# Gates of the last two token chunks by seven half-block products

## The chip, the cores and the metric

The kernel runs on one core of one Trainium2 chip. The metric is device microseconds (us) of one execution, taken as the median over runs; 255.19 us before the change. Engines are named as the profile names them: PE is TensorE (its weight loads have a row of their own, PEld), DVE is VectorE, ACT is ScalarE, POOL is GpSimd, SP is SyncE, which here only issues transfers.

## The reference

Linear attention over 8 batches of 8 heads, 576 positions and 64 features, followed by a gated feed-forward block over all 4608 tokens:

```
def phi(x):
    return np.where(x > 0, x, np.exp(x) - 1.0) + 1.0
kv  = einsum('bhsd,bhse->bhde', phi(k), v)
z   = sum(phi(k), axis=2)
num = einsum('bhsd,bhde->bhse', phi(q), kv)
den = einsum('bhsd,bhd->bhs', phi(q), z)[..., None] + 1e-06
x   = (num / den) as 4608 tokens x 512
a = x @ w1          # 512 -> 1024
b = x @ w2          # 512 -> 1024
h = a * b @ w3      # 1024 -> 1024
out = h @ w_out     # 1024 -> 512
```

Inputs and output are float32; the kernel multiplies in bf16 and accumulates in float32.

## The kernel before

The product w3 @ w_out is formed once on the chip (tile `wf_sb`), so that behind the gates a * b only one matrix is left. The tokens are treated in nine chunks of 512. Chunk c below 8 holds positions 0 to 511 of batch c; chunk 8 holds the remaining 64 positions of all eight batches ("the tails"). For each chunk there are these steps:

- K, `kv_full`: batch b's kv product, accumulated in PSUM and copied to SBUF by ACT or DVE.
- A, `nat`: the numerators and denominators of 128 tokens (j = 0 to 3), or of the 64 tail positions (j = 4): four matmuls of 130 columns into the one PSUM tile `nd`, then on DVE an addition, a reciprocal and a multiplication into `xn` or `xnr`.
- D, `xt_load`: a transposing transfer, issued by SP, that turns `xn` into `xt` (feature rows, token columns), or a pair of batches' `xnr` into a quarter of `xtr`, which chunk 8 reads.
- F, `f_unit`: one of eight column blocks of 128 gates: four matmuls of 512 columns with w1 into `a_ps` (L343), four with w2 into `b_ps`, an ACT copy of `a_ps` (L348) and a DVE multiplication with `b_ps` into `ab` (L349).
- O, `o_unit`: 128 output tokens: eight matmuls of 512 columns (L500) and a copy by ACT, or by DVE where the step has a plus (L502).
- S and H, stores of two output blocks or one; Q, `o_last`: the last block in two halves of 256 columns (L525), each copied and stored on its own.

What follows what is not left to a scheduler. A string, ORDER, lists all steps; the program is recorded in that order, every engine works through its own instructions in it, and the waits between engines follow from the data and from the reuse of buffers. A plus behind a step moves its copy or its operation to another engine. Transfers are queued on SP and POOL in the same order.

PSUM has eight banks here: four of tag "mm" (the F steps, Q), one each of tags "o" and "u" (the O steps take turns), and two for the tile that `nat` and `kv_full` share. SBUF tiles of tag "ld" (13 buffers of 4 KB per partition) take the loads of k, q and v; behind batch 7's conversion nothing loads into them any more.

The kernel before already has functions for gates by seven products (`ws_make`, `xs_make`, `g_product`, `g_unit`, `g_mul`; steps e, d, G and m), but its ORDER does not use them.

Of the kernel before, what the change touches and what calls it, by code (L numbers as in the profile page):

```python
# [8 lines left out]
F32 = mybir.dt.float32  # L9
BF16 = mybir.dt.bfloat16  # L10
AF = mybir.ActivationFunctionType
ALU = mybir.AluOpType

P = 128
NCH = 512
HN = 256
NQ = 4
# [3 lines left out]
def kernel(  # L21
# [11 lines left out]
    nc = tc.nc  # L33
# [15 lines left out]
    ld = ctx.enter_context(tc.tile_pool(name="ld", bufs=13))  # L49
# [4 lines left out]
    lr = ctx.enter_context(tc.tile_pool(name="lr", bufs=4))  # L54
    xt_p = ctx.enter_context(tc.tile_pool(name="xt", bufs=3))
    ab_p = ctx.enter_context(tc.tile_pool(name="ab", bufs=2))
    ws_p = ctx.enter_context(tc.tile_pool(name="ws", bufs=1))
    sm = ctx.enter_context(tc.tile_pool(name="sm", bufs=3))
    mm_ps = ctx.enter_context(tc.tile_pool(name="mm_ps", bufs=4, space=bass.MemoryType.PSUM))
    o_ps_p = ctx.enter_context(tc.tile_pool(name="o_ps", bufs=1, space=bass.MemoryType.PSUM))  # L60
# [250 lines left out]
    def xt_of(c):  # L311
        if c == B:
            return xtr
        if c not in xts:
            xts[c] = xt_p.tile([P, NJ, KC, P], BF16, tag="xt", name="xt")
        return xts[c]
# [40 lines left out]


    wss, xss, cs_ = [[None] * 4, [None] * 4], {}, {}

    def ws_make(w, i, alt):
        t, s = (w1_sb, w2_sb)[w], wss[w]
        s[i] = ws_p.tile([P, 2, NQ * P], BF16, tag=f"w{w}{i}", name=f"ws{w}{i}")

        def blk(r, h):
            return t[:, 2 * h:2 * h + 2, r * NCH:r * NCH + NQ * P]
        a, b, op = ((lambda: blk(1, 0), lambda: blk(1, 1), ALU.add),
                    (lambda: s[0], lambda: blk(0, 0), ALU.subtract),
                    (lambda: blk(0, 0), lambda: blk(1, 0), ALU.subtract),
                    (lambda: blk(0, 1), lambda: s[1], ALU.subtract))[i]  # L370
        (nc.gpsimd if alt else nc.vector).tensor_tensor(out=s[i], in0=a(), in1=b(), op=op)

    def xs_make(c, i, alt):
        if c not in xss:
            xss[c] = xt_p.tile([P, 4, 2, 2, P], BF16, tag="xs", name="xs", bufs=1)
        x, s = xt_of(c), xss[c]

        def blk(h, r):
            return x[:, 2 * r:2 * r + 2, 2 * h:2 * h + 2]
        a, b = ((lambda: blk(0, 1), lambda: blk(0, 0)), (lambda: blk(1, 1), lambda: s[:, 0]),  # L380
                (lambda: blk(1, 1), lambda: blk(0, 1)), (lambda: blk(1, 0), lambda: s[:, 1]))[i]
        (nc.gpsimd if alt else nc.vector).tensor_tensor(
            out=s[:, i], in0=a(), in1=b(), op=ALU.subtract)

    def g_product(t, c, q, a, m, first):

        for w in range(2):
            for k in range(2):
                if a[0] == 0:
                    l = (w1_sb, w2_sb)[w][:, 2 * a[2] + k, (q + 4 * a[1]) * P:(q + 4 * a[1] + 1) * P]  # L390
                else:
                    l = wss[w][a[1]][:, k, q * P:(q + 1) * P]
                if m[0] == 0:
                    r = xt_of(c)[:, 2 * m[2]:2 * m[2] + 2, 2 * m[1] + k, :]
                else:
                    r = xss[c][:, m[1], :, k, :]
                nc.tensor.matmul(t[:, w], l, r, start=(first and w == 0 and k == 0), stop=(k == 1),
                                 skip_group_check=True)

    def fsm(name):  # L400
        return sm.tile([P, 2, HN], F32, tag="f", name=name, bufs=4)

    def g_unit(c, q, i):
        if c not in abs_:
            abs_[c] = ab_p.tile([P, FC, NCH], BF16, tag="ab", name="ab")
        st = cs_.setdefault((c, q), {})
        a, m, name, first = ((), ((0, 0, 0), (0, 0, 0), "u", True), ((0, 0, 1), (0, 1, 0), "t", True),
                             ((1, 1), (1, 1), "u", False), ((1, 0), (1, 0), "t2", True),
                             ((1, 2), (1, 2), "u", False), ((1, 3), (0, 1, 1), "t2", False),
                             ((0, 1, 1), (1, 3), "u", False))[i]  # L410
        if first:
            pool, tag = (o_ps_p, "ou"[q % 2]) if name == "u" else (mm_ps, "mm")
            st[name] = pool.tile([P, 2, HN], F32, tag=tag, name="g" + name)
        t = st[name]
        g_product(t, c, q, a, m, first)
        if i in (1, 3, 4):
            s = st["s", i] = fsm("gs")
            nc.scalar.copy(out=s, in_=t)
        elif i in (2, 5, 6):
            s = st["c", i] = fsm("gc")  # L420
            nc.vector.tensor_tensor(out=s, in0=st["s", {2: 1, 5: 4, 6: 3}[i]], in1=t, op=ALU.add)
        else:
            s = fsm("ga")
            nc.scalar.copy(out=s[:, 0], in_=t[:, 0])
            nc.vector.tensor_mul(out=abs_[c][:, q + 4, 0:HN], in0=s[:, 0], in1=t[:, 1])

    def g_mul(c, q, i, alt):
        s = cs_[c, q]["c", i]
        f, r = {2: (q, 0), 5: (q + 4, 1), 6: (q, 1)}[i]
        (nc.gpsimd if alt else nc.vector).tensor_mul(  # L430
            out=abs_[c][:, f, r * HN:(r + 1) * HN], in0=s[:, 0], in1=s[:, 1])


    def a_block(c, r, h):
# [124 lines left out]
    x6.0 M7.0 A5.3 D3.1 x7.0 z6.1 F4.0 v6.1+ v6.2 F4.6 A4.4 Z6.0 F4.1 S3.0 F4.4 D5.0 A5.4 y6.0 z6.0  # L559
    F4.3 M7.1 F5.7 x7.2 y7.0 Y7.0 z7.2 L7.1 N7.0 K6+ z7.0 F5.6 F5.0 y7.1 X7.1 X7.0 Z7.0 F5.5 S3.1  # L560
    F5.3 Y7.1 T6.0 R7.1+ Z7.1 A6.3 T7.0 F5.1 O4.2 A6.1 x7.1 O4.1 A6.2 N7.1 z7.1 F5.4 A6.0 F5.2 v7.1
    v7.2+ O4.0 D6.0 D5.1 A6.4 v7.0 O4.3+ S4.1 K7 O5.0 F6.3 S4.0 O5.1 A7.4 F6.5 F6.4 D7.1 F6.1 A7.3
    O5.2 O5.3 A7.1 F6.2 F8.3 A7.0 F8.6 S5.1 F6.6 A7.2 S5.0 F6.0 F6.7 D7.0 O6.3+ O6.2 O6.1 O6.0+ F7.1
    F7.7 F7.2 F8.0 S6.1 F8.7 S6.0 F8.1 F8.5 F7.4 F8.2 F8.4 F7.6 O8.2 F7.5 H8.2 F7.3 F7.0 O8.3 H8.3
    O7.0 O7.1 S7.0 O8.0 O8.1 S8.0 O7.2 H7.2 Q7.3
    """
    GATES = "R6.0<T3.0"
    ctx.enter_context(tc.manual_schedule())
# [8 lines left out]
    def step(s):  # L577
# [5 lines left out]
        if t == "F":  # L583
            f_unit(b, i)
        elif t == "G":
            g_unit(b, i, int(at[1]))
        elif t == "m":
            g_mul(b, i, int(at[1]), alt)
        elif t == "e":
            ws_make(b, i, alt)  # L590
        elif t == "d":
            xs_make(b, i, alt)
        elif t == "O":
            o_unit(b, i, alt)
# [89 lines left out]
```

## Time and profile before

| what | value |
|---|---|
| median of three runs | 255.19 us |
| lowest and highest of them | 254.96 and 255.96 us |
| the profiled execution: time on the device | 254.38 us |
| the profiled execution: span of the profile | 252.6 us |
| transfers in the profiled execution | 49.54 MB, 196 GB/s on average |

The span runs from the first instruction to the end of the last transfer. The 1.8 us between it and the execution's own time lie around the profile. A profile's matmul lasts longer than the distance to the next one, since matmuls are pipelined: what a matmul costs is read from the distance of starts. All rows with a line number (L343) refer to the kernel before.

### The profile page before, as it was taken

To read this page: it belongs to the slowest core of one execution; us is meant where nothing else is said; L and a number is where in the kernel's file an instruction comes from. 1 tells how busy PE (TensorE), PEld (TensorE's weight loads), DVE (VectorE), ACT (ScalarE), POOL (GpSimd) and SP (SyncE) were. 2 spreads that over 40 slices of the span, in tenths; PEclk is the share of its full clock that TensorE was granted. 3 is DMA by queue.
4 is the path that set the end of the run, shared out by engine and by line. 5 is a ranking of instruction groups with operands and counts; after the bars stand their busy time and mean duration, and the time that the engine had idled before them with its cause. 6 is when DMAs were issued, how large, how long until landed. Compare 5 with 4: busy or idle time off the path is not lost.

```text
span 252.6 us, 3848 instructions
## 1 busy us (share of the span) xinstructions
PE 231.3 (92%) x1384; PEld 117.8 (47%) x1400; DVE 156.9 (62%) x350; ACT 116.1 (46%) x179; POOL 48.7 (19%) x82
## 2 busy tenths in 40 slices
PE   0088999999999999998999999999999999999994
PEld 0064564654454544444445445444544444444442
DVE  0548498679998566967886999887235632442300
ACT  2402677357756636719471573645232312323231
POOL 8625469456041050600000000000000000000000
PEclk9999999999999999999999999999999999999999
DMA  6999999999999999999999999656512244000144
GB/s 219 213 229 214 295 272 185 204 255 283 292 232 297 198 273 293 277 274 264 342 303 256 302 219 298 128 98 154 197 23 82 84 84 169 0 0 3 39 149 145
DMA packets 65427, 49.54 MB, mean 196 GB/s; under 512 B 33536, under 2 KB 60416, under 8 KB 65408
## 3 DMA queue, kind: packets, MB, share of 16 engines
q1 hardware_dynamic: 54576, 37.10, 58.6%
q0 software_dynamic: 10688, 12.06, 23.8%
q8 instruction: 11, 0.18, 0.3%
q10 hardware_dynamic: 144, 0.13, 0.1%
q14 instruction: 8, 0.07, 0.1%
HBM read 38.80 MB, written 9.44 MB: 191 GB/s over the span
## 4 chain that ended last, share of the span: by engine, by line
PE 69%; DMA 21%; issue 3%; SPq 2%; DVE 2%; POOL 1%; ACT 1%; ACTq 0%; POOLq 0%
PE a_ps L343 21%; PE b_ps L343 21%; PE o_ps L500 20%; DMA w3b<-in_moe_w_dram 10%; DMA q<-in_q_dram 5%; DMA v<-in_v_dram 3%; PE nd L301 3%; DMA qk32r<-in_k_dram 3%; PE kvp L246 2%; SPq L105 1%; SPq L332 1%; PE o_ps L525 1%; DVE kj L210 1%; PE kvp L250 1%; PE kvp L240 0%
## 5 line engine op out<-in xcount | busy, mean ns | idle before, releaser
L343 PEld LDWEIGHTS <-w_sb 128*128 128x128 bf16 x576 | 55.0, 98 | 63.2 <-issue 1.9
L349 DVE TENSOR_TENSOR ab<-a_sb,b_ps 128x512 bf16<-128x512 f32 x72 | 49.2, 686 | 38.4 <-PE b_ps L343 28.9
L343 PE MATMUL a_ps<-xt,w_sb 128*128 128x512 bf16 x256 | 66.7, 379 | 0.7 <-ACT xt L323 0.5
L343 PE MATMUL b_ps<-xt,w_sb 128*128 128x512 bf16 x256 | 66.7, 379 | 0.2 <-DVE ab L349 0.2
L348 ACT COPY a_sb<-a_ps 128x512 f32<-128x512 f32 x72 | 42.0, 585 | 53.7 <-PE a_ps L343 49.2
L500 PE MATMUL o_ps<-wf_sb,ab 128*128 128x512 bf16 x267 | 62.7, 379 | 0.8 <-issue 0.2
L500 PEld LDWEIGHTS <-ab 128*128 128x128 bf16 x280 | 26.9, 98 | 29.9
L502 ACT COPY o_sb<-o_ps 128x512 f32<-128x512 f32 x29 | 16.8, 586 | 41.8 <-PE o_ps L500 26.4
L307 DVE TENSOR_TENSOR xn<-nd,r 128x512 bf16<-128x512 f32 x32 | 22.1, 691 | 1.1
L180 ACT ACTIVATE e<-k 128x1024 bf16<-128x1024 f32 x16 | 16.6, 1055 | 7.8 <-DMA k<-in_k_dram 7.8
L180 ACT ACTIVATE e<-q 128x1024 bf16<-128x1024 f32 x16 | 16.7, 1055 | 7.4 <-DMA q<-in_q_dram 7.4
L148 PE MATMUL w3p<-ident,w3b 128*128 128x128 bf16 x64 | 5.7, 242 | 13.3 <-DMA w3b<-in_moe_w_dram 13.3
L301 PEld LDWEIGHTS <-qt 128*128 128x128 bf16 (+1 forms) x160 | 11.5, 99 | 11.4 <-issue 2.7
L301 PE MATMUL nd<-kv,qt 128*128 128x130 bf16 (+1 forms) x160 | 15.8, 220 | 0.5 <-ACT kv L255 0.5
L185 DVE TENSOR_SCALAR y<-q 128x1024 bf16<-128x1024 f32 x16 | 11.0, 694 | 8.0 <-DMA q<-in_q_dram 8.0
L155 PE MATMUL wf_ps<-wt_sb,w3t 128*128 128x512 bf16 x61 | 14.8, 379 | 0.7 <-DMA wt_sb<-in_moe_w_out_dram 0.5
L305 DVE TENSOR_SCALAR r<-nd 128x8 f32<-128x8 f32 (+1 forms) x40 | 6.4, 161 | 13.2 <-PE nd L301 12.8
L115 POOL DMA_DIRECT2D qk32r<-in_q_dram x14 | 9.0, 648 | 24.9 <-DMA qt<-qj 11.9
L210 DVE TENSOR_TENSOR qj<-e,y 128x512 bf16<-128x512 bf16 x32 | 12.0, 418 | 0.4 <-ACT e L180 0.3
L185 DVE TENSOR_SCALAR y<-k 128x1024 bf16<-128x1024 f32 x16 | 11.0, 687 | 2.0 <-DMA k<-in_k_dram 1.9
L210 DVE TENSOR_TENSOR kj<-e,y 128x512 bf16<-128x512 bf16 x32 | 11.9, 418 | 0.2
L148 PEld LDWEIGHTS <-w3b 128*128 128x128 bf16 x64 | 4.5, 109 | 14.8 <-DMA w3b<-in_moe_w_dram 14.5
(59 smaller groups left out, 181.7 us busy)
## 6 DMA issues: line engine op xcount, KB each, us to landing
out_dram<-o_sb SPq DMA_DIRECT2D x15, 512.0 KB, 3.7
q<-in_q_dram SPq DMA_DIRECT2D x13, 512.0 KB, 9.2
k<-in_k_dram SPq DMA_DIRECT2D x13, 512.0 KB, 6.4
v<-in_v_dram SPq DMA_DIRECT2D x12, 512.0 KB, 8.9
w3b<-in_moe_w_dram POOLq DMA_DIRECT2D x8, 256.0 KB, 12.2
w_sb<-in_moe_w_dram POOLq DMA_DIRECT2D x8, 256.0 KB, 7.2
q<-in_q_dram POOLq DMA_DIRECT2D x3, 512.0 KB, 11.4
k<-in_k_dram POOLq DMA_DIRECT2D x3, 512.0 KB, 12.4
```

The source lines that it names most:

```text
L148: nc.tensor.transpose(tp[:, kc, :], raw["w3", i // 4][:, i % 4, kc * P:(kc + 1) * P], ident)
L155: nc.tensor.matmul(wfs[i], w3ts[i][:, kc, :], wo_sb[:, kc, :], start=(kc == 0), stop=(kc == FC - 1))
L180: nc.scalar.activation(out=e, in_=x, func=AF.Exp)
L185: (nc.gpsimd if alt else nc.vector).tensor_scalar(out=y, in0=x, scalar1=0.0, scalar2=1.0, op0=ALU.max, op1=ALU.add)
L210: nc.vector.tensor_tensor(out=p[0][:, 2 * g + c].rearrange("p j u d -> p u j d"), in0=e[:, c], in1=y[:, c], op=ALU.min)
L301: nc.tensor.matmul(nd[rows, g, i * 2 * E1:(i + 1) * 2 * E1], w, kvs[b % 2][:, i, g].rearrange("p u e -> p (u e)"), start=True, stop=True)
L307: nc.vector.tensor_tensor(out=dst.rearrange("p (g h) e -> p g h e", g=2), in0=v4[:, :, :, 0:D], in1=r[rows].unsqueeze(3).to_broadcast([n, ...
L343: nc.tensor.matmul(ps, w[:, kc, f * P:(f + 1) * P], xt_of(c)[:, :, kc, :], start=(kc == 0), stop=(kc == KC - 1))
L348: nc.scalar.copy(out=a_sb, in_=a_ps)
L349: nc.vector.tensor_mul(out=abs_[c][:, f, :], in0=a_sb, in1=b_ps)
L500: nc.tensor.matmul(o_ps, ab[:, f, m * P:(m + 1) * P], wf_sb[:, f, :], start=(f == 0), stop=(f == FC - 1))
L502: copy_of(alt)(out=rows_of(c, m // 2)[:, m % 2], in_=o_ps)
```

## The change

The 16 F steps of chunks 7 and 8 are replaced by steps G. With the 1024 gate columns split into two halves of 512, the 512 features into two halves of 256 and the 512 tokens into two halves of 256, a gate matrix is a product of two 2 x 2 block matrices; seven block products with sums of blocks (Strassen, in Winograd's form) give it instead of eight. `g_unit(c, q, i)` does product i (1 to 7) for the column blocks q and q + 4, for w1 and w2 together: 2 x 2 matmuls of 256 columns into one bank. Products 1, 3 and 4 are copied to SBUF by ACT, products 2, 5 and 6 are added on DVE to such a copy, product 7 ends in an ACT copy of the w1 half and a DVE multiplication by the w2 half. `g_mul` (step m) multiplies the two halves of the sums 2, 5 and 6 on DVE. Products 3, 5 and 7 go on accumulating in the bank of product 1, and product 6 in that of product 4.

Steps e form the sums of weight blocks (four each of w1 and w2, 1024 bf16 columns), steps d the sums of xt blocks (four for each of the two chunks, 512 columns); all of them on DVE.

The buffers for these come from the pool of the loads: four tiles for the weight sums, two for the xt sums, and six tiles cut in two for a ring of twelve float32 buffers. Their order of reuse is written out with `ring`.

```
-    ws_p = ctx.enter_context(tc.tile_pool(name="ws", bufs=1))
...
+    spare = {}
+
+    def from_ld(key, shape, dtype):
+        if key not in spare:
+            spare[key] = ld.tile(shape, dtype, tag="ld", name="spare")
+        return spare[key]
...
-        s[i] = ws_p.tile([P, 2, NQ * P], BF16, tag=f"w{w}{i}", name=f"ws{w}{i}")
+        s[i] = from_ld(("w", w, i // 2), [P, 2, 2, NQ * P], BF16)[:, i % 2]
...
-            xss[c] = xt_p.tile([P, 4, 2, 2, P], BF16, tag="xs", name="xs", bufs=1)
+            xss[c] = from_ld(("x", c), [P, 4, 2, 2, P], BF16)
...
+    ring = []
+
     def fsm(name):
-        return sm.tile([P, 2, HN], F32, tag="f", name=name, bufs=4)
+        if not spare.get("ring"):
+            spare["ring"] = True
+            for n in range(6):
+                t = from_ld(("f", n), [P, 2, 2, HN], F32)
+                ring.extend((t[:, 0], t[:, 1]))
+        return ring.pop(0)
...
-            nc.vector.tensor_tensor(out=s, in0=st["s", {2: 1, 5: 4, 6: 3}[i]], in1=t, op=ALU.add)
+            o = st["s", {2: 1, 5: 4, 6: 3}[i]]
+            nc.vector.tensor_tensor(out=s, in0=o, in1=t, op=ALU.add)
+            ring.append(o)
```

A buffer also goes back to the ring behind product 7's multiplication and behind each step m. The order of the steps, from the store S4.1 on; before:

```
S4.1 K7 O5.0 F6.3 S4.0 O5.1 A7.4 F6.5 F6.4 D7.1 F6.1 A7.3
O5.2 O5.3 A7.1 F6.2 F8.3 A7.0 F8.6 S5.1 F6.6 A7.2 S5.0 F6.0 F6.7 D7.0 O6.3+ O6.2 O6.1 O6.0+ F7.1
F7.7 F7.2 F8.0 S6.1 F8.7 S6.0 F8.1 F8.5 F7.4 F8.2 F8.4 F7.6 O8.2 F7.5 H8.2 F7.3 F7.0 O8.3 H8.3
O7.0 O7.1 S7.0 O8.0 O8.1 S8.0 O7.2 H7.2 Q7.3
```

and after:

```
S4.1 e0.0 K7 F6.1 e0.2 O5.0 e0.1 e1.2 S4.0 A7.4 D7.1 e1.0
O5.1 F6.0 d8.0 A7.3 e1.1 O5.2 O5.3 d8.1 d8.2 d8.3 A7.2 G8.0.1 e0.3 G8.1.4 G8.1.1 G8.0.2 e1.3
G8.0.4 G8.0.3 G8.1.3 F6.6 G8.0.5 G8.1.5 m8.0.2 m8.1.5 G8.0.6 F6.5 m8.0.6 G8.1.7 G8.0.7 F6.7
m8.0.5 G8.2.1 G8.3.1 G8.1.6 G8.2.4 G8.2.3 A7.1 G8.3.3 G8.3.4 G8.2.5 S5.1 F6.4 A7.0 G8.3.5 G8.2.7
F6.2 m8.1.6 S5.0 D7.0 G8.3.7 F6.3 m8.3.5 G8.3.6 O6.0+ G8.3.2 d7.0 m8.3.6 O6.1+ d7.1 m8.2.5 d7.3
O6.2+ d7.2 O6.3+ G7.0.1 S6.0 G8.2.6 G8.1.2 G7.1.1 m8.2.6 G7.0.4 m8.1.2 G7.0.3 G7.1.2 G7.1.3
G7.1.4 m8.3.2 G7.0.5 G7.1.5 G7.2.4 S6.1 G8.2.2 G7.0.7 G7.1.7 G7.1.6 G7.0.2 m8.2.2 G7.2.1 G7.3.1
m7.1.2 G7.0.6 m7.1.6 G7.2.3 G7.2.2 G7.3.3 G7.2.5 G7.3.4 G7.3.2 G7.3.5 G7.2.7 G7.3.6 G7.2.6
G7.3.7 m7.0.2 O8.0+ m7.3.2 m7.2.2 O8.1 O8.2 S8.0 O8.3+ m7.0.5 m7.1.5 H8.2 m7.0.6 m7.2.6 m7.3.5
m7.2.5 H8.3 m7.3.6 O7.0 O7.1+ O7.2+ S7.0 H7.2 Q7.3
```

The instructions of every engine ahead of this point are the same in both programs.

More of the change, by code (lines that the diff above doesn't have):

```diff
@@ L425, in g_unit @@
             nc.vector.tensor_mul(out=abs_[c][:, q + 4, 0:HN], in0=s[:, 0], in1=t[:, 1])
+            ring.append(s)
     def g_mul(c, q, i, alt):
@@ L431, in g_mul @@
             out=abs_[c][:, f, r * HN:(r + 1) * HN], in0=s[:, 0], in1=s[:, 1])
+        ring.append(s)
     def a_block(c, r, h):
@@ L561 @@
     F5.3 Y7.1 T6.0 R7.1+ Z7.1 A6.3 T7.0 F5.1 O4.2 A6.1 x7.1 O4.1 A6.2 N7.1 z7.1 F5.4 A6.0 F5.2 v7.1
[L562 to L565, printed above, removed]
+    v7.2+ O4.0 D6.0 D5.1 A6.4 v7.0 O4.3+ S4.1 e0.0 K7 F6.1 e0.2 O5.0 e0.1 e1.2 S4.0 A7.4 D7.1 e1.0
+    O5.1 F6.0 d8.0 A7.3 e1.1 O5.2 O5.3 d8.1 d8.2 d8.3 A7.2 G8.0.1 e0.3 G8.1.4 G8.1.1 G8.0.2 e1.3
[7 more added lines that the diff above has]
+    m7.2.5 H8.3 m7.3.6 O7.0 O7.1+ O7.2+ S7.0 H7.2 Q7.3
     """
```

## The prediction

> **What bounds the kernel now.** I read the page first, then the stretches behind batch 7's kv product, then the chain of waits, then single instructions in order of time.
>
> ```profile
> span 252.6 us, 3848 instructions
> PE 231.3 (92%) x1384; PEld 117.8 (47%) x1400; DVE 156.9 (62%) x350; ACT 116.1 (46%) x179; POOL 48.7 (19%) x82
> ...
> PE   0088999999999999998999999999999999999994
> ...
> DVE  0548498679998566967886999887235632442300
> ...
> PEclk9999999999999999999999999999999999999999
> ```
>
> TensorE (PE) is the full engine from the third slice to the last, and the clock granted is whole all along. VectorE (DVE) falls from 8 and 9 tenths to 2 to 6 tenths from slice 28 (177 us) on. That is where the change begins: the order of steps is the same up to batch 7's kv product (K7), whose last product ends at 178.4 us. Behind that point, in four stretches (columns: bounds, length, then PE, PEld, DVE, ACT, POOL busy us with counts, clock, DMA share, GB/s):
>
> ```profile
> 178.00:189.00 11.00, 10.95 (x60) 5.17 (x59) 3.29 (x7) 3.98 (x8) 0.00 (x0) 1.00 0.30 109
> 189.00:212.00 23.00, 22.89 (x118) 10.95 (x119) 10.17 (x21) 6.16 (x12) 0.00 (x0) 1.00 0.29 92
> 212.00:231.00 19.00, 18.95 (x89) 8.60 (x89) 7.57 (x11) 6.36 (x11) 0.00 (x0) 1.00 0.07 28
> 231.00:249.00 18.00, 17.95 (x91) 8.73 (x90) 2.49 (x4) 5.86 (x10) 0.00 (x0) 1.00 0.34 93
> ```
>
> PE is busy 70.7 of 71 us, while DVE does 23.5 us of work and ACT 22.4. So PE's time in this stretch is the time of the kernel, and a microsecond taken off PE comes off the end, as long as nobody makes it wait. The chain of waits (start, length, what) says the same and prices the products:
>
> ```profile
> 211.00 0.86 PE a_ps L343 x4
> 211.87 0.86 PE b_ps L343 x4
> ...
> 228.27 0.86 PE a_ps L343 x4
> ...
> 247.26 1.76 PE o_ps L525 x16
> ```
>
> From 211.00 to 228.27 us lie 20 groups of four 512-column matmuls back to back: 17.27 / 80 = 0.2159 us each.
>
> **PE's sum.** Removed: sixteen F steps (F7.0 to F7.7, F8.0 to F8.7) of eight 512-column matmuls, 128 x 0.2159 = 27.63 us. Added: for two chunks, four column blocks and seven products, 2 x 2 matmuls of 256 columns, so 224, each with a weight load of its own (224 loads for 128). The 256-column matmul has rows in the last step, Q7.3 (start, length, engine; the length of one is 0.272):
>
> ```profile
> 246.88 1.84 PEld L525 LDWEIGHTS <-ab 128*128 128x128 bf16 x16
> 247.10 1.91 PE L525 MATMUL o_ps<-wf_sb,ab 128*128 128x256 bf16 x16
> ...
> L525 PE MATMUL o_ps<-wf_sb,ab 128*128 128x256 bf16 x16 | 1.9, 272 | 0.0
> L525 PEld LDWEIGHTS <-ab 128*128 128x128 bf16 x16 | 1.6, 98 | 0.4
> ```
>
> Sixteen take 1.91 us, so (1.91 - 0.272) / 15 = 0.1092 us each, with a weight load of 98 ns between each two. 224 x 0.1092 = 24.46. PE's work shrinks by 27.63 - 24.46 = **3.17 us**; by the chain's coarser 1.76 / 16 = 0.110 it would be 2.99.
>
> A load of 98 ns beside a product of 109 leaves little room, so this is the place to ask whether loads are hidden. The rows above say they are; so does a narrower case:
>
> ```profile
> 189.21 0.39 PE L301 MATMUL nd<-kv,qt 128*128 128x130 bf16 x4
> 189.38 3.17 PEld L500 LDWEIGHTS <-ab 128*128 128x128 bf16 x16
> 189.44 3.62 PE L500 MATMUL o_ps<-wf_sb,ab 128*128 128x512 bf16 x15
> ```
>
> Four 130-column products and their four loads pass in 189.44 - 189.21 = 0.23 us, 58 ns a pair. I take loads as free; if they were not, 96 more of them at 98 ns would cost 9.4 us (a rival below). The Trainium skill, page "TensorE: Matmul & The Clock Gate", section "Part 3: Packing small matmuls — row/col tiling", under "The mechanism", says that a weight load overlaps running matmuls only where the two use different row groups; all of these use the full array, so by it every load would stand in series. The two fences disagree with it.
>
> **What the seven products ask of DVE and ACT.** A removed F step has one ACT copy and one DVE product of 128x512, 16 of each. Added per column block: three ACT copies and three DVE adds of 128x512, an ACT copy and a DVE product of 128x256 from PSUM, and three DVE products of 128x256 in SBUF. Their prices:
>
> ```profile
> 166.53 0.69 DVE L307 TENSOR_TENSOR xn<-nd,r 128x512 bf16<-128x512 f32 x1
> 167.14 0.68 DVE L349 TENSOR_TENSOR ab<-a_sb,b_ps 128x512 bf16<-128x512 f32 x1
> ...
> 181.00 0.59 ACT L502 COPY o_sb<-o_ps 128x512 f32<-128x512 f32 x1 [1.63 <-DMA out_dram<-o_sb]
> 181.48 0.59 ACT L348 COPY a_sb<-a_ps 128x512 f32<-128x512 f32 x1
> ...
> 248.23 0.42 DVE L527 COPY o_sb<-o_ps 128x256 f32<-128x256 f32 x1 [10.53 <-DMA out_dram<-o_sb]
> 249.05 0.37 ACT L527 COPY o_sb<-o_ps 128x256 f32<-128x256 f32 x1 [1.12 <-PE o_ps L525]
> ```
>
> A DVE operation of 512 columns lasts 0.69 us, but the next starts after 167.14 - 166.53 = 0.61; ACT's after 0.48. The add has no row (f32 out instead of bf16), nor has the f32 product of two SBUF operands. I price the add like L349: 0.61 in a queue, 0.69 alone. For the 256-column products the nearest row is L527's copy: 0.42 alone, and with the same overlap of 0.08, 0.34 in a queue. The lower end for them is half of that (0.21), the upper end twice (0.85).
>
> Per column block DVE needs 3 x 0.61 + 4 x 0.34 = 3.2 us, and PE 28 x 0.1092 = 3.06. So DVE, idle for two thirds of this stretch before, becomes as costly as PE wherever products follow each other undiluted. ACT needs 3 x 0.48 + 0.29 = 1.7 and has room.
>
> Chunk 8's products are mixed with six F6 steps and two nat steps. From A7.2 to O6.0 the new order has 24 of the 28 products (24 x 4 x 0.1092 = 10.5 us) and 48 + 8 older products (6 x 1.73 + 2 x 0.23 = 10.8), 21.3 us on PE; DVE has 8 adds, 10 small products, 6 L349 and two nat chains of 1.1, with two weight sums: 4.9 + 3.4 + 3.7 + 2.2 + 1.2 = 15.4. It is hidden.
>
> Chunk 7's are not diluted: from G7.0.1 to O8.0 PE has 31 products, 31 x 4 x 0.1092 = 13.54 us, DVE 15 adds, 4 products from PSUM and 7 deferred ones: 15 x 0.61 + 11 x 0.34 = 12.9 us, 95% of PE's. With every operation at its full length it is 15 x 0.69 + 11 x 0.42 = 15.0, and PE would wait 1.4. Each add holds a bank that a later product needs, so at this load some waits come through. Bounds 0 and 1.4; I take 0.3, near the lower end, because the spacing of 0.61 is what back-to-back rows show.
>
> The remaining nine small products of chunk 7 stand on DVE behind O8.0's copy; seven of them behind O8.3's, which waits for PE to finish O8.3. O7.2 reads what they write. From the end of O8.3, DVE needs 0.61 + 7 x 0.34 = 3.0 us and PE gives it O7.0 and O7.1, 2 x 1.73 = 3.45. Cover 0.45; at 0.42 each, 0.1 of a wait; at 0.85 each, 3.1. I take 0.15.
>
> The sums of weights (eight of 1024 columns, bf16) and of xt blocks (eight of 512) go to DVE. For bf16 sums of 512 columns the row is
>
> ```profile
> L210 DVE TENSOR_TENSOR qj<-e,y 128x512 bf16<-128x512 bf16 x32 | 12.0, 418 | 0.4 <-ACT e L180 0.3
> ```
>
> so between 0.42 and 0.84 each for the longer ones, at most 8 x 0.84 + 8 x 0.42 = 10 us in 41 us (178 to 219) where DVE had about 16 us of work before; the six weight sums ahead of chunk 8's first products lie under F6.1, F6.0 and four O5 steps. At nothing, with one exception.
>
> **The step that moves past a queue.** DVE works strictly in order, and d8.0 (first sum of tail blocks) waits there for batch 7's tail transpose, D7.1; behind it stands A7.3's normalisation, and PE's A7.2 waits for that, since nat has one PSUM tile. The rows of before:
>
> ```profile
> 178.40 1.89 PE L500 MATMUL o_ps<-wf_sb,ab 128*128 128x512 bf16 x8
> ...
> 183.68 0.41 PE L301 MATMUL nd<-kv,qt 128*64 128x130 bf16 x4
> ...
> 184.13 0.17 DVE L305 TENSOR_SCALAR r<-nd 64x8 f32<-64x8 f32 x1 [1.31 <-PE nd L301]
> ...
> 184.56 0.69 DVE L307 TENSOR_TENSOR xnr<-nd,r 64x512 bf16<-64x512 f32 x1
> ...
> 185.28 1.19 SPq L332 DMA_TRANSPOSE xtr<-xnr  x1
> ...
> xtr<-xnr SPq DMA_TRANSPOSE x1, 2.4
> ...
> DMA to landing us min/median/max: 2.4/4.4/7.5
> ```
>
> In the new order F6.1 starts at 178.40, A7.4 after two steps of 1.73 at 181.9. DVE is through with F6.1's product at about 180.9 and then has three weight sums, to 182.8; A7.4's chain of 1.15 lets SP issue D7.1 at 184.0, 1.3 us earlier than before. With a landing of 2.4 us d8.0 starts at 186.4 and A7.3's chain ends near 188.0. PE reaches A7.2 after six steps of 1.73 and two of 0.23, at 178.4 + 10.8 = 189.2. So a landing of up to about 3.5 us is covered, and each microsecond beyond it is a microsecond of PE. I take 2.4, the row of this same transfer with the queue quiet around it; S4's two stores stand ahead of D7.1 as before. D7.0, the last xt transpose, is issued some 5 us later than before, behind S5's stores, and still has about 6 us before the first chunk 7 sum is read. Nothing else on SP or POOL moves past a wait that matters.
>
> **Sum.** Against the profiled execution's own time, 254.38 us (its span of 252.6 and 1.8 around it): 254.38 - 3.17 + 0.3 + 0.15 = 251.7. The median of the runs, 255.19, stands 0.8 above that execution, so I forecast **252.5 us**, and 251.7 to 253.9 for this case alone (no wait at all and some noise; up to 1.9 us of waits).
>
> **Rivals.**
> First, VectorE sets the pace of chunk 7's gates. With x more per add the stage costs PE 15x - 0.6 us. For it: 95% load, and add and SBUF product without rows. Against it: L349, with the same operands but the output's type, and the 0.61 spacing. At x = 0.18 to 0.33 the waits reach 2 to 4.4 us and the result lies within 0.5% (0.5%, 1.28 us, is about what a measurement of this kernel can tell from no change): about 255. Slower than before it becomes from x = 0.25, clearly so from 0.33; at 0.4 the stage loses 5.4 and the time is 255.19 - 3.17 + 5.4 = 257.4.
> Second, D7.1 lands late. Two of four such transposes took over 4.4 us, up to 7.5, but while loads ran; here the loads are over. At 7.5 the wait is 4.0 and the time 256.5; it decides against the change from a landing of 6.2.
> Third, weight loads stand in series: 255.19 - 3.17 + 9.4 = 261.4. Both fences speak against it.
> That the change doesn't reach the path is no rival: PE is busy 70.7 of 71 us there, and the products are on it.
>
> **How the numbers follow.** Forecast 0.74. VectorE half way, within 0.5%: 0.12; VectorE clearly: 0.05. D7.1 late: 0.05, of it 0.02 within 0.5%, 0.03 slower. Loads in series: 0.02. A small SBUF product at twice its price or more: 0.02, slower. So faster 0.74, same 0.14, slower 0.12. The range goes from 251.7 to 255.4: the forecast's own and most of VectorE's middle case.
>
> **What would show it.** In the new profile: 224 matmuls of 256 columns at 109 ns spacing; PE without a gap over 0.3 us between 178 and 246; D7.1 issued near 184 and landed by 187; DVE at 9 tenths from 219 to 234 us; the add at 0.69 and the SBUF product at about 0.42. I am wrong if the add lasts over 0.8, the SBUF product over 0.6, or PE's gaps in front of chunk 7's products sum to over 2 us.

## The result and the profile after

| | median of runs, us | lowest to highest |
|---|---|---|
| before, beside it | 255.07 (4 runs) | 254.93 to 255.96 |
| after | 252.55 (4 runs) | 251.09 to 252.72 |

The ratio is 0.9881, with a 95% interval of 0.9838 to 0.9924: faster by 1.2%, and by more than 0.5% over the whole interval. The profiled execution of after took 252.62 us, its span is 250.6.

The stretches behind K7 in the profile after (columns as before; these are 2 us shorter at the end):

```profile
178.00:189.00 11.00, 10.95 (x69) 5.69 (x69) 7.30 (x15) 3.10 (x6) 0.00 (x0) 1.00 0.39 126
189.00:212.00 23.00, 23.00 (x165) 15.37 (x163) 16.99 (x38) 12.53 (x24) 0.00 (x0) 1.00 0.22 66
212.00:231.00 19.00, 18.95 (x144) 13.95 (x143) 16.65 (x34) 7.25 (x14) 0.00 (x0) 1.00 0.16 60
231.00:247.00 16.00, 15.87 (x90) 8.72 (x89) 9.77 (x22) 2.64 (x6) 0.00 (x0) 1.00 0.37 101
```

PE is as full as before, and DVE's work has grown from 23.5 us to 50.7. In order of time, the end of K7, the two ends of chunk 7's stage, and the end:

```profile
179.54 1.03 PE L342 MATMUL a_ps<-xt,w_sb 128*128 128x512 bf16 x4
...
219.44 0.60 PE L402 MATMUL gu<-xt,w_sb 128*128 128x256 bf16 x4
219.64 0.69 DVE L518 COPY o_sb<-o_ps 128x512 f32<-128x512 f32 x1 [0.70 <-PE o_ps L516]
...
220.51 1.29 DVE L434 TENSOR_TENSOR spare<-spare,gt 128x512 f32<-128x512 f32 x2 [0.18 <-PE gt L402]
...
222.76 0.69 DVE L434 TENSOR_TENSOR spare<-spare,gt 128x512 f32<-128x512 f32 x1 [0.30 <-PE gt L402]
...
224.07 1.28 DVE L434 TENSOR_TENSOR spare<-spare,gu 128x512 f32<-128x512 f32 x2 [0.29 <-PE gu L402]
...
226.16 0.85 DVE L439 TENSOR_TENSOR ab<-spare,gu 128x256 bf16<-128x256 f32 x2 [0.15 <-ACT spare L438]
...
232.97 12.25 PE L516 MATMUL o_ps<-wf_sb,ab 128*128 128x512 bf16 x54
...
234.19 0.42 DVE L445 TENSOR_TENSOR ab<-spare 128x256 bf16<-128x256 f32 x1
...
240.08 0.69 DVE L518 COPY o_sb<-o_ps 128x512 f32<-128x512 f32 x1 [3.82 <-PE o_ps L516]
240.69 2.43 DVE L445 TENSOR_TENSOR ab<-spare 128x256 bf16<-128x256 f32 x7
...
245.06 1.91 PE L541 MATMUL o_ps<-wf_sb,ab 128*128 128x256 bf16 x16
```

The first matmul behind K7 starts at 179.54 us, Q7.3 at 245.06: 65.52 us, where before had 247.10 - 178.40 = 68.70. The difference is **3.18 us**. I call this distance "the stretch" from here on, because all that the change touches lies in it. PE has no wait in it: G7.0.1 starts at 219.44, O8.0 at 232.97, so 31 products took 13.53 us, and the O steps follow as one block. DVE's waits between its operations of chunk 7's stage (in brackets, from 220.51 to 226.16 us) are short and add up to 0.92 us. With 0.20 us at the start of the stage, ahead of O6.3's copy at 219.64, and two gaps too short for a row, DVE idled 1.17 of the 13.53 us.

What the new operations cost (mean in ns behind the comma):

```profile
L434 DVE TENSOR_TENSOR spare<-spare,gt 128x512 f32<-128x512 f32 x16 | 10.7, 683 | 0.8 <-PE gt L402 0.7
L445 DVE TENSOR_TENSOR ab<-spare 128x256 bf16<-128x256 f32 x24 | 9.2, 417 | 0.0
...
L439 DVE TENSOR_TENSOR ab<-spare,gu 128x256 bf16<-128x256 f32 x8 | 3.3, 417 | 0.2 <-ACT spare L438 0.2
...
L376 DVE TENSOR_TENSOR spare<-w_sb 128x1024 bf16<-128x1024 bf16 x4 | 2.7, 686 | 0.0
```

But the profiled execution as a whole is shorter by 254.38 - 252.62 = 1.76 us only. K7's last products are 1.14 us later (first matmul behind K7 at 179.54 against 178.40), and ahead of them both programs have the same instructions; the other 0.28 us lies behind Q7.3 and around the span. Rows of before:

```profile
99.98 3.91 SPq L332 DMA_TRANSPOSE xt<-xn  x1
...
116.28 0.63 PE L246 MATMUL kvp<-vt,kj 128*128 128x130 bf16 x8 [0.88 <-DVE kj L210]
```

and of after:

```profile
100.04 1.02 PE L342 MATMUL b_ps<-xt,w_sb 128*128 128x512 bf16 x4 [0.89 <-DVE ab L348]
...
101.06 4.94 SPq L331 DMA_TRANSPOSE xt<-xn  x1
...
110.05 1.04 PE L342 MATMUL a_ps<-xt,w_sb 128*128 128x512 bf16 x4 [1.30 <-DMA xt<-xn]
...
117.42 0.62 PE L245 MATMUL kvp<-vt,kj 128*128 128x130 bf16 x8
```

In after, PE waits 1.30 us for batch 3's transposed tile, a wait that before has not. It doesn't explain the 1.14 us, though. After was 1.08 us late already when this transpose was issued (101.06 against 99.98), and from there to K4's first matmul it is 16.36 us with the wait and 16.30 without, since before waits 0.88 us for batch 4's k in front of K4 instead. Whether the lateness belongs to the change was the first question for the experiments.

### The profile page after: what moved, and what is told of

It reads as the page before. It is cut to its first block, busy times and chain, and to the rows that moved or that the text cites. A ratio compares the mean times of both kernels' runs of the same rounds, so it can differ in the third digit from the quotient of the medians.

```text
span 250.6 us, 4124 instructions
## 1 busy us (share of the span) xinstructions
PE 228.2 (91%) x1481; PEld 127.1 (51%) x1496; DVE 184.2 (74%) x412; ACT 119.2 (48%) x189; POOL 48.5 (19%) x82
## 4 chain that ended last, share of the span: by engine, by line
PE 54%; DMA 7%; ACT 1%; issue 0%; ACTq 0%
PE o_ps L516 18%; PE a_ps L342 11%; PE b_ps L342 11%; PE gu L402 6%; PE gt L402 4%; DMA xt<-xn 4%; DMA v32r<-in_v_dram 3%; PE nd L300 2%; PE kvp L245 1%; PE o_ps L541 1%; ACT e L179 0%; PE kvp L249 0%; ACT o_sb L543 0%; ACT a_sb L347 0%; ACTq L543 0%
## 5 line engine op out<-in xcount | busy, mean ns | idle before, releaser
L342 PEld LDWEIGHTS <-w_sb 128*128 128x128 bf16 x448 | 42.6, 98 | 49.4 <-issue 2.2
L342 PE MATMUL a_ps<-xt,w_sb 128*128 128x512 bf16 x224 | 58.5, 379 | 1.9 <-DMA xt<-xn 1.3
L342 PE MATMUL b_ps<-xt,w_sb 128*128 128x512 bf16 x224 | 58.5, 379 | 1.0 <-DVE ab L348 0.9
L348 DVE TENSOR_TENSOR ab<-a_sb,b_ps 128x512 bf16<-128x512 f32 x56 | 38.2, 684 | 18.1 <-PE b_ps L342 12.6
L347 ACT COPY a_sb<-a_ps 128x512 f32<-128x512 f32 x56 | 32.5, 585 | 31.8 <-PE a_ps L342 29.9
L518 ACT COPY o_sb<-o_ps 128x512 f32<-128x512 f32 x23 | 13.3, 586 | 35.4 <-PE o_ps L516 17.6
L147 PE MATMUL w3p<-ident,w3b 128*128 128x128 bf16 x64 | 5.7, 242 | 13.3 <-DMA w3b<-in_moe_w_dram 13.3
L430 ACT COPY spare<-gu 128x512 f32<-128x512 f32 x16 | 9.1, 591 | 11.7 <-PE gu L402 11.5
L518 DVE COPY o_sb<-o_ps 128x512 f32<-128x512 f32 x12 | 8.3, 691 | 8.5 <-PE o_ps L516 8.0
L402 PEld LDWEIGHTS <-spare 128*128 128x128 bf16 x128 | 12.4, 98 | 1.8
## 6 DMA issues: line engine op xcount, KB each, us to landing
q<-in_q_dram SPq DMA_DIRECT2D x13, 512.0 KB, 10.8
```

Of the source, the lines that this page charges most:

```text
L342: nc.tensor.matmul(ps, w[:, kc, f * P:(f + 1) * P], xt_of(c)[:, :, kc, :], start=(kc == 0), stop=(kc == KC - 1))
L347: nc.scalar.copy(out=a_sb, in_=a_ps)
L348: nc.vector.tensor_mul(out=abs_[c][:, f, :], in0=a_sb, in1=b_ps)
L518: copy_of(alt)(out=rows_of(c, m // 2)[:, m % 2], in_=o_ps)
```

## The experiments

Each starts from the changed kernel. Where only a profile was taken, the stretch is the measure; where times were taken, the ratio to before has its interval.

**The same kernel again, twice.** No edit.

> The changed kernel once more, nothing edited, to part what the change does from what differs between executions ahead of batch 7's kv product, where both programs have the same instructions at the same addresses. Measured by the stretch from K7's last product to the start of Q7.3 (before 68.70 us, after 65.52 us). Theory (all of the gain is PE's shorter work behind K7; the 1.1 us by which K7 came later in the profile of after is chance): the stretch is 65.5 us again within 0.2, K7 starts anywhere between 176.5 and 178.5 us, and the median of the runs is 251.5 to 252.7. Rival (the change makes the part ahead of K7 slower): K7 starts after 178 us again and the median stays above 252.3.

> The changed kernel unedited, on the same chip, as the measure for the run before. Both theories: stretch 65.5 us, median 251.5 to 252.7 us.

Measured: stretch 65.52 us in both, to the hundredth what the first profile had. Median 251.86 us (ratio 0.9863, 0.9821 to 0.9905) and 252.33 us (0.9869, 0.9823 to 0.9915). K7 started at 177.6 us in both. In the first of them the trace holds every matmul, and PE is busy without a break (columns as above, 178 to 244 us):

```profile
178.00:189.00 11.00, 11.00 (x67) 5.51 (x65) 7.92 (x17) 3.68 (x7) 0.00 (x0) 1.00 0.31 110
189.00:212.00 23.00, 23.00 (x165) 15.40 (x164) 17.01 (x38) 11.95 (x23) 0.00 (x0) 1.00 0.24 69
212.00:231.00 19.00, 19.00 (x148) 14.24 (x147) 16.65 (x34) 7.39 (x14) 0.00 (x0) 1.00 0.14 56
231.00:244.00 13.00, 13.00 (x68) 6.44 (x66) 7.86 (x18) 2.51 (x5) 0.00 (x0) 1.00 0.35 81
```

The gain behind K7 is fixed; what comes ahead of K7 differs from execution to execution. In the thirteen profiles with the old place of F3.7 (before, after and eleven experiments, the same instructions up to there) batch 3's transpose landed 6.8 to 10.7 us after its issue. Four times, at 6.8 to 7.7 us, PE waited nothing; at 8.2 it waited 0.6, at 8.9 to 9.1 (six times) 1.3 to 1.5, at 9.9 2.1, at 10.7 3.0 us. Before and after happened to get 7.6 and 8.9. The theory held, the rival fell.

Waits of up to 1.5 us for this tile are not what moves K7. In ten of the eleven profiles with a landing of up to 9.1 us, K4's first matmul comes 16.1 to 16.5 us behind the transpose's issue, whether PE waited for the tile or not: where it waited little or nothing, it waited 0.5 to 1.1 us for batch 4's k in front of K4. With the landings of 9.9 and 10.7 us it is 17.3 and 20.9 us. From K4 to K7 the distance is 61.0 us in all profiles but two (61.1 and 61.3). What else differs ahead of the transpose's issue, at 99.4 to 101.5 us, is open.

**Chunk 8 alone.** Chunk 7 by F steps at the places of its products 1 and 4; no d7, no m7.

```
-G7.0.1 ... G7.0.4 ...
+F7.0 ... F7.4 ...
```

> Only chunk 8's gates by seven products; chunk 7's by the F steps of before, at the places of the new order. Theory (each chunk gives 64 x 0.2159 - 112 x 0.1092 = 1.59 us, no waits): the stretch from K7's last product to Q7.3 is 68.70 - 1.59 = 67.1 us, the time about 253.5 us. Rival (the gain is mostly the new order, or mostly chunk 7's): the stretch stays at 65.5 to 66, or at 68 or more.

Measured: stretch 67.11 us, 1.59 less than before; median 253.49 us, ratio 0.9948 (0.9909 to 0.9987). Theory, to the hundredth. Its two ends:

```profile
179.08 1.03 PE L342 MATMUL a_ps<-xt,w_sb 128*128 128x512 bf16 x4
...
246.19 1.91 PE L541 MATMUL o_ps<-wf_sb,ab 128*128 128x256 bf16 x16
```

**The order alone.** F steps in both chunks, no sums.

```
-e0.0 ... G8.0.1 ... G8.1.4 ... G7.0.1 ...
+F8.0 ... F8.5 ... F7.0 ...
```

> The new order of the steps behind K7 with F steps in the places of products 1 and 4, without sums, products 2, 3, 5, 6, 7 and steps m. Theory (the order gives nothing, since PE had no gap to fill): the stretch is 68.5 to 69.2 us, the time within 0.3% of before. Rival (the order gives a part of the gain): the stretch is below 68 us.

Measured: stretch 69.08 us, median 256.04 us, ratio 1.0026 (0.9992 to 1.0060). The order gives nothing; without the products it even has one wait, 0.21 us in front of an O6 step, by the distance of starts 0.37.

**Chunk 7 alone.** Chunk 8 by F steps, no d8, no m8.

```
-G8.0.1 ... G8.0.4 ...
+F8.0 ... F8.4 ...
```

> Only chunk 7's gates by seven products; chunk 8's by F steps at the places of products 1 and 4. By the count of work alone (from G7.0.1 to O8.0 PE has 28 products, 12.2 us, and DVE fewer adds than before, about 10 us) nothing waits and the stretch is 67.1 us. Rival (in the changed kernel chunk 8's last products stand between products of chunk 7 that share a bank; without them the next product of a bank comes before ACT or DVE has read the last one): waits of 1 to 1.5 us in chunk 7's stage, the stretch 68 to 68.5 us.

Measured: stretch 68.30 us; a gain of 0.39 instead of 1.59. The rival was right. Two of the waits, in order of time:

```profile
215.95 6.43 PE L516 MATMUL o_ps<-wf_sb,ab 128*128 128x512 bf16 x29 [0.20 <-DVE ab L348]
...
222.22 0.60 PE L402 MATMUL gu<-xt,w_sb 128*128 128x256 bf16 x4
222.42 0.69 DVE L518 COPY o_sb<-o_ps 128x512 f32<-128x512 f32 x1 [0.70 <-PE o_ps L516]
...
223.16 0.60 PE L402 MATMUL gu<-xt,w_sb 128*128 128x256 bf16 x4 [0.35 <-DVE o_sb L518]
```

G7.1.1 starts 0.94 us behind G7.0.1 instead of 0.44, because its bank still holds O6.3, which DVE copies until 223.11. In the changed kernel two of chunk 8's products, G8.2.6 and G8.1.2, stand between them. The 0.20 above is 0.37 by the distance of starts, as in the order alone: O6.0 waits for F6.3's product, and in both runs G8.3.6, which the changed kernel has between F6.3 and O6.0, is missing. Two smaller waits at 227.2 and 227.8 us bring the sum to 1.2. So the two chunks' gains don't add up from single runs: chunk 8's G8.2.6 and G8.1.2 cover chunk 7's second product, and G8.3.6 covers O6.0. What the two smaller waits are for is open.

**More work for DVE in chunk 7's stage.** An extra product of constants behind each of chunk 7's twelve adds, its result unused:

```
             ring.append(o)
+            if c == 7:
+                nc.vector.tensor_mul(out=extra[:, 0:N], in0=wf_sb[:, 0, 0:N], in1=wf_sb[:, 1, 0:N])
```

N = 128:

> One extra DVE product of 128 bf16 columns (about 0.14 us in a queue, result unused) behind each of chunk 7's twelve adds: 1.7 us more DVE work in the stretch from G7.0.1 to O8.0, which has 13.54 us of PE work and by count 12.9 of DVE work. Theory (DVE is at 95% there and becomes the limit as soon as its work passes PE's): PE waits about 1 us, and the stretch from K7's last product to Q7.3 grows from 65.5 to 66.3 to 66.9. Rival (DVE has much more room than the count says): no growth over 0.3 us.

N = 512:

> The same with 512 bf16 columns (about 0.34 us in a queue): 4.1 us more DVE work. Theory: 12.9 + 4.1 - 13.5 = 3.5 us of waits (up to 4), the stretch 68.5 to 69.5 us, so the gain of the change is gone. Rival (room): the stretch grows by less than 2 us.

Measured: stretches 66.15 and 68.23 us, so PE lost 0.63 and 2.71. The small one took this much of DVE's queue (start, length):

```profile
229.34 0.68 DVE L435 TENSOR_TENSOR spare<-spare,gt 128x512 f32<-128x512 f32 x1
229.93 0.22 DVE L438 TENSOR_TENSOR extra<-wf_sb 128x128 bf16<-128x128 bf16 x1
230.07 0.68 DVE L435 TENSOR_TENSOR spare<-spare,gu 128x512 f32<-128x512 f32 x1
```

An extra operation holds the queue 0.14 us, twelve 1.7, and PE lost 0.63: DVE had 1.0 us of room. With 4.1 us more it lost 2.71, a room of 1.4. My expectations (0.8 to 1.4, and 3.5) were built on a room of 0.6 from the count; both results lie below, and both stretches just under those expected (66.3 to 66.9, and 68.5 to 69.5). The theory that DVE becomes the limit holds, with a somewhat larger room.

The N = 512 run's time, 259.64 us, can't be read as the price of the edit: ahead of K7 its execution had the late transpose of 10.7 us.

**The ring's order.** `ring.pop()` in place of `ring.pop(0)`.

> The ring of twelve float32 buffers hands out the buffer given back last instead of the one given back first; all else as in the changed kernel. Theory (the twelve buffers and the order of their reuse are what lets ACT's and DVE's work of several products lie in flight, so PE doesn't wait): waits of 3 to 7 us come in, of ACT for DVE and of PE for both, and the stretch is 68.5 to 72 us. Rival (PSUM banks and the order of the steps alone set the pace): the stretch stays below 66.5 us.

Measured: stretch 71.21 us, 5.7 us of waits; the longest in a row of three:

```profile
229.75 0.75 DVE L445 TENSOR_TENSOR ab<-spare 128x256 bf16<-128x256 f32 x2
230.26 1.07 ACT L430 COPY spare<-gu 128x512 f32<-128x512 f32 x2 [2.46 <-DVE ab L445]
...
230.90 0.60 PE L402 MATMUL gu<-spare 128*128 128x256 bf16 x4 [1.56 <-ACT spare L430]
```

The copy wants the buffer that DVE has just read, ACT waits 2.46 us for it, and PE waits for ACT. One argument of one call costs more than the whole change brings.

**The tail later.** A7.4 and D7.1 behind F6.0, d8.0 and A7.3 behind O5.2 (run twice), and A7.4 with D7.1 behind O5.1 only.

```
-A7.4 D7.1 e1.0 O5.1 F6.0 d8.0 A7.3 e1.1 O5.2 O5.3
+e1.0 O5.1 F6.0 A7.4 D7.1 e1.1 O5.2 d8.0 A7.3 O5.3
...
-A7.4 D7.1 e1.0 O5.1 F6.0
+e1.0 O5.1 A7.4 D7.1 F6.0
```

> Batch 7's tail (A7.4 and its transpose D7.1) two PE steps later, behind F6.0, and d8.0 with A7.3 one step later: the first sum of tail blocks waits longer on DVE, with A7.3's normalisation behind it. Theory (d8.0 stands in DVE's queue, and A7.2 waits behind it, with a cover of 1.2 to 1.3 us in the changed kernel): D7.1 is issued 3.4 us later, and PE waits about 2 us in front of A7.2, so the stretch grows from 65.5 to between 67.3 and 68. Rival (DVE's wait for the transpose is hidden anyway): no wait of PE over 0.5 us, a stretch of 65.5 to 66.

> The kernel with the tail two steps later once more, unedited; there D7.1 took 4.0 us to land instead of 2.4, PE waited 3.5 us, the clock granted fell to half for some 6 us and the stretch was 72.1 us. Theory (a wait of PE long enough lowers the clock, and that doubles its price): with a landing near 2.4 us the wait is about 2 us and the stretch 67.5 to 68.5 with a whole clock; with a landing near 4 us again the wait is about 3.5 us, the clock falls again and the stretch is 71.5 to 72.5. Rival (the low clock was chance): a wait of 3 us or more with a whole clock, the stretch near 69 us.

> A7.4 and D7.1 one PE step later than in the changed kernel (behind O5.1) instead of the more than two of the run before, to find where the cover of d8.0's wait ends without a long wait of PE. Theory (cover of 1.35 us in the changed kernel, two DVE sums less in front of A7.4's chain, D7.1 issued 1.2 to 1.7 us later, landing 2.4 us): PE waits 0 to 0.4 us, the clock granted stays whole, the stretch from K7's last product to Q7.3 is 65.5 to 65.9 us. Rival (the long stretch of the other run came from the new place of D7.1 among the stores, not from the length of the wait): the stretch is above 67 us.

Measured, two steps later: stretch 72.10 us, and 70.09 when repeated, far over the expected 67.3 to 68. The wait is there, behind d8.0 as the theory has it, and with it the granted clock falls (a row of PE, then columns as above; the third number from the right is the clock, and 0.91 and 0.74 are means over a whole and a half one):

```profile
193.22 0.61 PE L300 MATMUL nd<-kv,qt 128*128 128x130 bf16 x4 [3.54 <-DVE xn L306]
```

```profile
185.00:189.00 4.00, 4.00 (x25) 1.83 (x24) 2.44 (x5) 0.89 (x2) 0.00 (x0) 1.00 0.08 17
189.00:193.00 4.00, 0.69 (x4) 0.10 (x1) 1.32 (x4) 0.59 (x1) 0.00 (x0) 0.91 0.88 195
193.00:197.00 4.00, 3.78 (x20) 2.83 (x21) 2.74 (x8) 1.74 (x3) 0.00 (x0) 0.50 0.22 87
197.00:201.00 4.00, 4.00 (x22) 2.49 (x20) 1.29 (x2) 2.34 (x5) 0.00 (x0) 0.74 0.00 0
201.00:205.00 4.00, 4.00 (x30) 2.73 (x28) 3.63 (x7) 0.84 (x3) 0.00 (x0) 1.00 0.00 0
```

D7.1 took 4.0 us to land, DVE waited 3.35 us for it and PE, in front of A7.2, 3.54. Of the 6.58 us that the stretch grew, 3.7 are the wait by the distance of starts, 2.9 the lower clock: PE worked at half of it for 5.9 us, from 193.2 to 199.1. In the repeat the landing was 3.5, the wait 3.03 (3.2 by the distance of starts), the clock at half from 192.8 to 196.2 us and whole again behind that, and 1.4 of 4.6 us were the clock's. One step later, D7.1 took 4.1 us, PE waited

```profile
191.66 0.40 PE L300 MATMUL nd<-kv,qt 128*128 128x130 bf16 x4 [1.30 <-DVE xn L306]
```

and the stretch was 67.00 us with a whole clock: the wait and nothing else (65.52 + 1.47 by the distance of starts). That is more than the 0 to 0.4 expected, because the transpose took 1.7 us longer to land than in its old place. It stands at the edge of the rival's mark (above 67 us), but the wait is what an issue 1.2 us later and a landing 1.7 us longer leave beyond the cover of 1.35, and the clock is whole. The repeat fell between the two cases that its expectation named, and with them the three runs say: a wait of 1.5 us costs itself, and one of 3 us or more costs more than itself.

One thing in the traces goes with the late landings. In the eleven profiles without this edit the transpose landed after 2.40 to 2.41 us, and its 544 packets were the only ones between its issue and its landing. In the three with a later tail a packet of 16 KB on the queue named "instruction" ran beside them. From issue to landing, in after (185.22 to 187.63 us) and one step later (186.04 to 190.12):

```profile
q1 hardware_dynamic: 544, 0.13, 27.3%
...
xtr<-xnr SPq DMA_TRANSPOSE x1, 2.4
```

```profile
q1 hardware_dynamic: 544, 0.13, 16.1%
q8 instruction: 1, 0.02, 1.3%
...
xtr<-xnr SPq DMA_TRANSPOSE x1, 4.1
```

In the eleven that packet comes 2.6 us or more behind the issue of D7.1, in the three 1.0 to 2.0 us behind it. That it holds the transpose up is likely, but no run tests it; in two of the three the stores of S5 were also issued before the landing.

**More cover for batch 3's transpose.** O2.2 moved in front of F3.7:

```
-O2.3 F3.7 ... Z5.0 S1.1 O2.2+ K4
+O2.3 O2.2+ F3.7 ... Z5.0 S1.1 K4
```

> The changed kernel with one output step (O2.2) moved from in front of K4 to in front of F3.7, the first step that reads batch 3's transposed tile; everything from K4 on is as in the changed kernel. In nine profiles so far, of eight programs that have the same instructions up to there, that transpose took 7.5 to 10.7 us to land and PE waited 0 to 3.0 us for it, 1.3 in four of them. Theory (this wait is what differs between executions ahead of K7): O2.2 gives 1.73 us of cover, the wait is gone up to a landing of about 9.4 us, the stretch from K7's last product to Q7.3 stays 65.5 us, and the median falls by about 1 us below the unedited kernel's of the same call (250.3 to 251.5 us). Rival (the time lost there comes back as another wait, of K4 or of a later transpose): the median is within 0.4 us of the unedited kernel's.

Measured: median 251.85 us, 0.48 below that of the unedited kernel measured beside it; ratio to before 0.9828 (0.9790 to 0.9867) against 0.9869 (0.9823 to 0.9915), so the two intervals overlap widely. The transpose took 9.4 us and PE didn't wait for it, but a little later for something else:

```profile
PE kvp L245 <- DVE kj L209: 1.6, 1, 1.6
```

K4 waits for batch 4's k on DVE, and K4's first matmul comes 16.85 us behind the transpose's issue, so in this profile all of the time won comes back there, as the rival said. The median lies outside both marks (250.3 to 251.5, and within 0.4 of the unedited kernel's); 0.5 us may stay, which these runs can't settle.

## Why the prediction was right, point by point

- **The time.** Forecast 252.5, measured 252.55, later 251.86 and 252.33. The ratios to before (0.9881, 0.9863, 0.9869) are falls of 3.0 to 3.5 us, around the 3.18 of the stretch. That the first median fits to a tenth is luck: 0.45 us of waits were added that didn't come, and the first two medians lie only 2.52 us apart (255.07 and 252.55), where the stretch gives 3.18. What was predicted rightly is the part behind K7.
- **PE's sum.** 3.17 us predicted, 3.18 measured; each chunk's share of 1.59 was measured by itself on chunk 8. Weight loads cost nothing: 31 x 4 matmuls in 13.53 us are 0.1091 us each, with a 98 ns load before every one. The rival with loads in series is gone.
- **VectorE's prices.** Predicted 0.69 for the add and 0.42 for the small products, both without a row; measured 0.683 and 0.417. The weight sums took 0.686, inside their bounds, and were hidden.
- **The waits in chunk 7's stage.** This term was mis-sized: 0.3 us predicted, none measured. The count of DVE's work, 12.9 us or 95% of PE's, was short as well: the 26 operations that it names took 13.3 us (from 220.51 to 234.61, less 0.8 of idle time), and O6.3's copy, 0.69 us in the same stage, was not in it. That makes 14.0 us of DVE's work beside 13.5 of PE's. No wait came all the same. The order suggests why, though no run tests it: the last 1.6 us of this work ran behind the start of O8.0, when no product was left to wait for a bank. By the extra work DVE's room was 1.0 to 1.4 us, where the count of PE's work less DVE's gave 0.6. The small-product queue in front of O7.2 was right (seven in 2.43 us), and its 0.15 of wait did not come either.
- **VectorE as the limit.** A rival with the right mechanism and nearly the right point: 4.1 us more work lost 2.7. What the prediction left out is that the load alone doesn't decide. With less DVE work but without chunk 8's late products, 0.8 us of waits came in between chunk 7's products and 0.4 in front of O6.0; with the same work and another order of buffers, 5.7 in all. The places of the products and the twelve buffers are part of what makes the gain possible.
- **D7.1 and d8.0.** D7.1 was predicted 5.6 us behind K7 and came at 185.22 - 179.54 = 5.68; it landed after 2.4 as before, and PE reached A7.2 11.0 us behind K7 (10.8 predicted) with A7.3's result 1.35 us old. The price in the rival, one microsecond for each beyond the cover, holds for short waits only: 1.47 us by the distance of starts one step later, but 4.6 us for a wait of 3.03 and 6.6 for one of 3.54. An estimate from these runs: with a cover of 1.35 us PE waits from a landing of 3.75 us on. At 5.9 us it would wait 2.1, which left the clock whole ahead of K7; at 6.8 us it would wait 3.0, which costs more than the change brings. The landing from which the change loses lies between the two, where the 6.2 us given also lie, and a landing of 7.5 us would have cost more than the 4.0 given.

## What to carry to other kernels

When one engine is full and another idle, count the trade stage by stage: here 3.2 us of PE were bought with 27 us of DVE, and the price is only right where DVE had 27 us to give. Here DVE's work in the densest stage was as long as PE's and still hidden. Chunk 7 alone and the ring's other order show what that hangs on: other work stands between two products that share a bank, and buffers are reused in the order in which they fall free. Test both, not the sum of durations alone. And compare executions by a stretch that begins behind the last common instruction: this one repeated to 0.01 us, while whole executions of the same program differed by up to 3.3.

## What was not expected of the hardware

A single wait of PE of 3.0 to 3.5 us, seen in three executions, brought the granted clock down to half, and there it stayed for 6.8, 3.4 and 6.8 us; in the two runs with the late tail 256-column matmuls then followed each other after 0.213 us instead of 0.109. So such a wait cost up to 1.9 times itself (6.58 us for 3.54). Waits of 0.6 to 2.1 us left the clock whole. The third of the long ones came ahead of K7, in the run with the large extra products, behind the 10.7 us transpose:

```profile
107.00:110.70 3.70, 1.71 (x8) 0.49 (x6) 3.51 (x10) 1.07 (x2) 0.00 (x0) 1.00 1.14 221
110.90:117.60 6.70, 5.90 (x17) 2.14 (x18) 2.62 (x6) 2.12 (x3) 0.00 (x0) 0.50 1.11 347
117.70:122.00 4.30, 4.30 (x23) 1.98 (x22) 3.28 (x8) 2.54 (x4) 0.00 (x0) 1.00 0.97 210
```

There K7 started at 182.9 us instead of 176.9 to 178.4. The Trainium skill, page "TensorE: Matmul & The Clock Gate", section "Part 1: The HAM clock gate (the "warmup" mystery)", says that the clock falls to half after an idle window of about 3.4 us in a free-running count. The runs agree on the half, and the low stretches are one or two times 3.41 us long. They differ on the idle window: waits of 3.0 us were enough, and the clock fell 2.1 to 2.6 us after PE had stopped, so the measured 3.0 us is what counts here; between 2.1 and 3.0 us no run has a wait.

The 22 runs of before on one chip took 252.9 to 259.5 us. Only the longest has a mean clock as low as the repeat of the late tail (0.992; the others 0.998 to 1.000). So a wait of this kind may lie behind that run, which was not profiled, but not behind the spread of the others, which reach 257.2 us.
